# Float32r products that read the two halves of each 128 moving columns in turn

## The chip, the cores and the metric

The kernel runs on one core of one Trainium2 chip. The metric is the device time of one execution in microseconds (us); less is better. TensorE (PE) multiplies, its weight loads are shown apart (PEld), VectorE (DVE), ScalarE (ACT) and GpSimd (POOL) work on elements, and transfers (DMA) are issued from the queues of SyncE (SP) and ScalarE.

## The reference

Sliding-window attention over 8 batches, 8 heads, 576 positions, 64 dimensions a head, followed by a two-layer network with a slope of its own for each hidden unit:

```python
def _attn_ref(q, k, v):
    scores = scale * np.matmul(q, k.transpose(0, 1, 3, 2))
    mask = (rel >= 0) & (rel < 64)
    ...
    return np.matmul(attn, v)

def _moe_ref(x, w_in, w_out, alpha):      # x: 4608 x 512, w_in: 512 x 2048, w_out: 2048 x 512
    h = x @ w_in
    g = np.maximum(h, 0.0) + alpha * np.minimum(h, 0.0)
    return g @ w_out
```

## The kernel before

The 4608 tokens are 36 tiles of 128, worked on in nine blocks of four tiles. Attention gives the tokens `x`, transposed (channels on partitions). The first product, `x @ w_in`, gives `h` with 128 hidden units on the partitions and a block's 512 tokens as columns, one hidden slice `f` of 16 at a time. ScalarE, VectorE and GpSimd make `g` of it. The second product takes 128 tokens of `g` as the stationary operand and a slice of `w_out` (512 output columns) as the moving one, and adds up a tile of the output in a PSUM bank over the 16 slices.

Each of the two operands of a product is held as a float32r number and a float32r rest (names ending in `h` and `l`), and a product is three float32r matmuls: high by high, high by low, low by high. The operands of attention are plain float32.

Five places issue float32r matmuls. `hidden` in `cell` (L1173) does the first product for blocks 0 and 1: twelve matmuls a slice, most of them with 512 moving columns (the tokens), a few with 256. `product` in `pair` (L1305) does it for the blocks behind, in a scheme with seven products of half size in place of eight: the moving operand is 256 tokens. `outs` in `behind` (L852) does the second product for all blocks but the last: 512 moving columns of `w_out`. `products` in `behind_last` (L1023) does the second product of the last block, again with seven products in place of eight, with 256 moving columns. In all of them the moving columns lie one behind the other in the partition's memory, and each matmul has a weight load of its own of 128 columns.

Finished tiles of the output go from PSUM to SBUF in `copy` (L894 on ScalarE, L896 on VectorE) and out in `store` (L899), 32 of them. The last block's four quarters are added up and moved in `quarter`: `make` (L1138 on ScalarE, L1140 on VectorE or GpSimd), with one store each from L1147 (two for the last one).

The order of the work on every engine is fixed ahead: `step` collects steps with their costs, `Plan.order` lays them out by costs and due times, and the instructions are issued in that order. Engines wait for each other by semaphores alone, so an engine that is done early goes on early. The costs in the plan are no part of the change.

Of the kernel before, what the change touches and what calls it, by code (L numbers as in the profile page):

```python
# [14 lines left out]
ALU = mybir.AluOpType  # L15
# [3 lines left out]
PE, DVE, ACT, POOL, SP = "PE", "DVE", "ACT", "POOL", "SP"  # L19
# [99 lines left out]
class Plan:  # L119
# [5 lines left out]
    def step(self, engines, emit, after=(), behind=(), take=(), give=(), want=math.inf, moved=0.0, span=0.0,  # L125
             port=False):

        s = Step(engines, emit, after, list(behind), list(take), list(give), want, moved, span, port)
        for a in s.after + s.behind:
            a.before.append(s)
        s.group = self.group
        self.steps.append(s)
        return s
# [152 lines left out]
def banded_attention_then_prelu_ffn(  # L289
# [11 lines left out]
    nc = tc.nc  # L301
    P = 128
    D = 64
    W = WINDOW
# [50 lines left out]
    def weight(name, f):  # L355
        f0 = max(x for x in parts_of[name] if x <= f)
        return parts_of[name][f0][:, f - f0, :]
# [5 lines left out]
    def tokens_of(x, where):  # L363
        half, start = divmod(where.start, NBLK * P)
        return xs_of[x, half][:, :, start:start + where.stop - where.start]
# [14 lines left out]
    nc.vector.memset(nought, 0.0)  # L380
    plan.idle = lambda _: nc.tensor.matmul(spare, nought, nought, start=True, stop=True)  # L381
    step = plan.step

    def bank(b, shape, dtype, name):
        return ps.tile(shape, dtype, tag=f"b{b.at}", name=name)
# [419 lines left out]
    po = {}  # L805
# [5 lines left out]
    def behind(ts, f, d, done, hb, want_o, cols, coarse=True):  # L811
        n = len(ts)
        nt = n * P
# [7 lines left out]
        start = ts[0] < NBLK  # L821
# [23 lines left out]
        def outs(todo):  # L845
            gh, gl = d["gh"], d.get("gl")
            for i, k in todo:
                t = ts[i]
                if f == 0 and k == 0:
                    po[t] = bank(ob[t], [P, E], F32, f"o_{t}")  # L850
                gt, wt = ((gh, "wout_h"), (gh, "wout_l"), (gl, "wout_h"))[k]
                nc.tensor.matmul(po[t], gt[:, cols[i] * P:(cols[i] + 1) * P], weight(wt, f),  # L852
                                 start=(f == 0 and k == 0), stop=(f == NF - 1 and k == 2))

        hold = {2: (1.46, 0.37, 0.40, 0.31, 0.69), 4: (2.72, 0.57, 0.667, 0.53, 1.24)}[n]
# [1 line left out]
        if f == 0:  # L857
            for t in ts:
# [5 lines left out]
                  give=[hb if start else gb])  # L864
# [3 lines left out]
        for todo in todos:  # L868
# [5 lines left out]
                      give=[ghb] + [glb] * lows, want=want_o)  # L874
# [5 lines left out]
        if f == NF - 1:  # L880
            apart = ts[0] // NBLK == W0 - 1
            if apart:
                old = [Buffer(f"x{i}", NBLK) for i in range(NBLK, RING)]
            for i, t in enumerate(ts):
                for x in parts(t):
                    sbuf, os = Buffer("g" if t == NT - 1 else "gh" if t == NT - 2 else "os", 1), {}

                    def copy(e, t=t, x=x, sbuf=sbuf, os=os, i=i):
                        if apart and not i:
                            lent_of["out"] = sb.tile([P, NP, NBLK * P], F32, tag="xh1", name="lent_out")  # L890
                        os[0] = (lent_of["out"][:, i] if apart else
                                 room(sbuf, [P, x.stop - x.start], F32, f"os_{t}_{x.start}"))
                        if e == ACT:
                            nc.scalar.copy(os[0], po[t][:, x])  # L894
                        else:
                            nc.vector.tensor_copy(os[0], po[t][:, x])  # L896

                    def store(e, t=t, x=x, os=os):
                        (nc.scalar if e == ACT else nc.sync).dma_start(out[t * P:(t + 1) * P, x], os[0])  # L899

                    m = len(parts(t))
                    c = step({DVE: (0.33, 0.42)} if x.start else {ACT: (0.28, 0.39)} if m == 2 else
                             {ACT: (0.48, 0.59), DVE: (0.6, 0.69)}, copy, [whole[t]],
                             [c] if apart and i else [], take=[] if apart and i else old if apart else [sbuf],
                             give=[ob[t]], want=want_o + 3 + i)
                    step({ACT: (0.4, 0.4)} if x.start else {SP: (0.4, 0.4)}, store, [c],
                         give=old if apart else [sbuf], moved=0.8 / m)
                    if t < NBLK:
                        begun.append(c)

    HALF = NF // 2
    entries_o, kept_o, slots, acc, mid = {}, {}, {}, {}, {}
# [49 lines left out]
    def behind_last(ts, f, d, done, hb, want_o, cols):  # L962
        n = NB - 1
        i = f % HALF
# [3 lines left out]
        lh, rh = slice(0, 2 * P), slice(2 * P, 4 * P)  # L968
# [47 lines left out]
        def products(name, kind, gh, gl, w):  # L1016
            fresh = name not in acc
            if fresh:
                acc[name] = bank(acc["b", name], [P, E], F32, f"acc_{name}")
            for j in range(2):  # L1020
                x, y = gh[:, j * P:(j + 1) * P], gl[:, j * P:(j + 1) * P]
                for k, (a, b) in enumerate(((x, w[0]), (x, w[1]), (y, w[0]))):
                    nc.tensor.matmul(acc[name][:, j * 2 * P:(j + 1) * 2 * P], a, b, start=fresh and j == k == 0,  # L1023
                                     stop=k == 2, skip_group_check=True)

        def product(name, kind, gh, gl, w, deps, give):
# [100 lines left out]
        u2 = step(wide, lambda _: sum_u("u2", None, lambda: acc["P6"], lambda: mid["P1"]), [p6], give=[acc["b", "P6"]], want=want_o)  # L1127
        u4 = step(wide, lambda _: sum_u("u4", fb, lambda: acc["P5"], lambda: u["u2"]), [p5, u2], take=[fb], give=[acc["b", "P5"]], want=want_o)
        def quarter(kind, rows, side, x, y, deps, want):
            many = 2 if x is last else 1  # L1130
            b, o = Buffer(kind, many), {}
            where = out[ts[0] * P:].rearrange("(j r p) c -> r p j c", j=2, r=2)[rows][:, :, side]

            def make(e):
                o[0] = room(b, [P, E], F32, f"quarter_{rows}_{side.start}").rearrange("p (j c) -> p j c", j=2)
                o[1] = o[0].rearrange("p j c -> p (j c)")
                if y is None:
                    nc.scalar.copy(o[1], x())  # L1138
                else:
                    (nc.gpsimd if e == POOL else nc.vector).tensor_tensor(out=o[1], in0=x(), in1=y(), op=ALU.add)  # L1140

            c = step({ACT: (0.48, 0.59)} if y is None else {POOL: (1.22, 1.28)} if x is u4_of else wide, make, deps, take=[b], want=want)
            for j in range(many):
                js = slice(j, j + 1) if many == 2 else slice(0, 2)

                def store(e, js=js):
                    (nc.scalar if e == ACT else nc.sync).dma_start(where[:, js], o[0][:, js])  # L1147

                step({ACT: (0.4, 0.4)} if j or rows and side is lh else {SP: (0.4, 0.4)}, store, [c], give=[b], moved=0.8 / many)
            return c  # L1150

        last, u4_of = lambda: acc["P1"], lambda: u["u4"]
# [7 lines left out]
    def cell(ts, f, want_h, want_o):  # L1160
        plan.group = "c", f, ts[0]
        n = len(ts)
        nt = n * P
        d = {}
        xs = slice((ts[0] % RING) * P, (ts[0] % RING) * P + nt)
        hb = Buffer("bank", 1)

        def hidden(_):
            d["h"] = ph = bank(hb, [P, NBLK * P], F32, f"h_{ts[0]}_{f}")
            k = 0  # L1170
            for wt, xt in (("win_h", "h"), ("win_h", "l"), ("win_l", "h")):
                for c in range(NP):
                    nc.tensor.matmul(ph[:, :nt], weight(wt, f)[:, c * P:(c + 1) * P], tokens_of(xt, xs)[:, c],  # L1173
                                     start=(k == 0), stop=(k == 3 * NP - 1))
                    k += 1

        xb = [st[t]["x"] for t in ts]
        s0 = step({PE: ({2: 1.46, 4: 2.72}[n], {2: 1.55, 4: 2.87}[n])}, hidden,
                  [st_done[t] for t in ts] + cv[2 * f]["done"], take=[hb], want=want_h)
        first[ts[0] // NBLK, f] = s0  # L1180
        for b in xb:
            b.uses = NF
        s0.give += xb
        if ts[0] // NBLK == W0 - 1:
            s0.give += regions[f // 2]
        behind(ts, f, d, [s0], hb, want_o, range(n), not (ts[0] // NBLK == W0 - 1 and f >= NF - 2))
# [79 lines left out]
    def pair(ts, q, want):  # L1266
        plan.group = "c", 2 * q, ts[0]
        n = ts[0] // NBLK
        f = 2 * q
# [31 lines left out]
        def product(out, w, x, start):  # L1301
            todo = [(w[i], x[j]) for i, j in ((0, 0), (0, 1), (1, 0))]
            for i, (a, b) in enumerate(todo):
                for c in range(2):
                    nc.tensor.matmul(out, a[:, c * P:(c + 1) * P], b[c], start=start and i == c == 0,  # L1305
                                     stop=i == 2 and c == 1, skip_group_check=True)

        def p12(_):
# [56 lines left out]
        cols = (0, 2, 1, 3)  # L1365
# [10 lines left out]
    for i, rooms in enumerate(TSETS):  # L1376
        b = Buffer(f"reg{i}", 3 * 6, f"T{i}")
# [54 lines left out]
    for n in range(2, NB + 1):  # L1432
        for i in (0, 1):
            m, f = (n - 1, STAYS[1] if n > 2 else 6) if i else (n - 2, STAYS[0]) if n > 2 else (1, 2)
# [93 lines left out]
```

## Time and profile before

| | us |
|---|---|
| three runs | 871.85, 869.1, 871.83 |
| median | 871.83 |
| span of the profiled execution | 869.5 |
| TensorE busy in it | 860.6 |
| VectorE, ScalarE, GpSimd busy | 596.0, 480.7, 425.4 |

The busy time of TensorE takes in the modelled ends of matmuls that overlap, so the rows that count are the times from one start to the next, which the chain of waits gives for a run of matmuls. The granted TensorE clock is 1.00 of its full 2.4 GHz.

### The profile page before, as it was taken

What the parts mean: (1) busy time and instruction counts of PE and PEld (TensorE: products, weight loads), DVE (VectorE), ACT (ScalarE), POOL (GpSimd) and SP (SyncE); (2) the same over time, 40 slices, a digit from 0 to 9 for tenths busy, and PEclk for the clock granted to TensorE, in tenths of its full rate; (3) what the DMA queues carried; (4) which work ended last, traced back from release to release, by engine and by line L of the source; (5) the groups of instructions that cost most, each with busy time, mean ns of one, the idle gap of its engine ahead of it and who ended that gap; (6) DMA issues with size and microseconds to landing.
All of it is one profiled execution on the core that took longest, in us unless ns stands there. A gap on an engine that the chain in (4) does not pass through costs nothing.

```text
span 869.5 us, 21449 instructions
## 1 busy us (share of the span) xinstructions
PE 860.6 (99%) x7937; PEld 765.4 (88%) x7937; DVE 596.0 (69%) x1683; ACT 480.7 (55%) x1290; POOL 425.4 (49%) x422
## 2 busy tenths in 40 slices
PE   9999999999999999999999999999999999999997
PEld 8887778888989898989899889989898989899997
DVE  6888978987775663877585678558776638425655
ACT  7888767447463534664554646364645446434542
POOL 5877656886333324646264435543353433222452
PEclk9999999999999999999999999999999999999999
DMA  9655846565665565766667575767676754367764
GB/s 317 209 185 176 257 162 215 161 213 184 224 183 182 144 190 183 226 188 191 207 184 229 170 241 144 238 179 223 185 230 171 214 185 138 107 204 227 230 202 158
DMA packets 128631, 170.75 MB, mean 196 GB/s; under 512 B 9728, under 2 KB 82448, under 8 KB 128528
## 3 DMA queue, kind: packets, MB, share of 16 engines
q1 hardware_dynamic: 127520, 168.47, 63.2%
q8 instruction: 63, 1.03, 0.5%
q10 hardware_dynamic: 1008, 0.93, 0.3%
q14 instruction: 40, 0.33, 0.1%
HBM read 141.04 MB, written 28.31 MB: 195 GB/s over the span
## 4 chain that ended last, share of the span: by engine, by line
PE 93%; DVE 2%; DMA 2%; ACT 1%; issue 0%; POOL 0%; ACTq 0%; DVEq 0%; SPq 0%; POOLq 0%
PE o L852 39%; PE h L1305 32%; PE h L1173 8%; PE acc_P L1023 4%; PE av L711 4%; PE s L590 3%; DMA raw<-w_in 1%; PE s L572 1%; PE spare L381 1%; DMA raw<-w_out 1%; PE t L668 1%; ACT two L414 0%; DVE two L424 0%; DVE val L433 0%; DVE two L416 0%
## 5 line engine op out<-in xcount | busy, mean ns | idle before, releaser
L835 POOL TENSOR_TENSOR gl<-g,gh 128x512 fp32r<-128x512 f32 x112 | 144.7, 1301 | 221.8 <-ACT gh L831 106.4
L852 PE MATMUL o<-wout_h,gh 128*128 128x512 f32 x512 | 203.4, 397 | 0.0
L852 PE MATMUL o<-wout_l,gh 128*128 128x512 f32 x512 | 201.5, 394 | 0.0
L818 ACT ACTIVATE g<-h,sa_sb 128x512 f32<-128x512 f32 (+1 forms) x132 | 89.2, 676 | 144.4 <-DVE h L1332 121.3
L852 PE MATMUL o<-wout_h,gl 128*128 128x512 f32 x512 | 142.0, 390 | 0.0
L691 DVE STREAM_TRANSPOSE pt<-w 32x256 f32<-32x256 f32 x312 | 128.2, 426 | 5.4 <-POOL w L651 0.7
L852 PEld LDWEIGHTS o<-wout_h,gl 128*128 128x128 f32 x512 | 95.3, 188 | 20.2
L852 PEld LDWEIGHTS o<-wout_h,gh 128*128 128x128 f32 x512 | 96.7, 189 | 17.2 <-issue 0.5
L852 PEld LDWEIGHTS o<-wout_l,gh 128*128 128x128 f32 x512 | 96.7, 189 | 15.1
L825 DVE SCALAR_TENSOR_TENSOR g<-h,s_sb,g 128x512 f32<-128x512 f32 x112 | 84.0, 750 | 37.8 <-ACT g L818 34.9
L1332 DVE TENSOR_TENSOR h<-h,w 128x256 f32<-128x256 f32 x56 | 24.2, 433 | 124.5 <-PE h L1305 124.5
L831 ACT CAST gh<-g 128x512 fp32r<-128x512 f32 x112 | 69.4, 621 | 49.1 <-DVE g L825 48.6
L630 ACT ACTIVATE w<-w,nm 128x96 f32<-128x96 f32 x208 | 76.1, 372 | 14.5 <-DVE nm L624 14.5
L1342 ACT COPY u<-h 128x256 f32<-128x256 f32 x112 | 41.8, 373 | 73.4 <-PE h L1305 69.5
L651 POOL TENSOR_TENSOR w<-w,rc 128x768 f32<-128x768 f32 (+2 forms) x44 | 59.3, 1347 | 46.0 <-DVE rc L647 40.5
L1305 PE MATMUL h<-xh,win_l 128*128 128x256 f32 x336 | 67.6, 283 | 0.0
L1305 PE MATMUL h<-xh,win_h 128*128 128x256 f32 x336 | 65.9, 283 | 0.0
L1305 PEld LDWEIGHTS h<-xh,win_h 128*128 128x128 f32 x336 | 56.7, 189 | 8.0 <-DVE h L1332 0.5
L1305 PE MATMUL h<-win_h,win_l 128*128 128x256 f32 x336 | 60.5, 283 | 0.0
L1332 DVE TENSOR_TENSOR h<-h,u 128x256 f32<-128x256 f32 x112 | 47.7, 428 | 15.8 <-PE h L1305 11.8
L1305 PEld LDWEIGHTS h<-xh,win_l 128*128 128x128 f32 x336 | 53.0, 191 | 0.8
L1305 PEld LDWEIGHTS h<-win_h,win_l 128*128 128x128 f32 x336 | 50.1, 190 | 0.9
(206 smaller groups left out, 1856.5 us busy)
## 6 DMA issues: line engine op xcount, KB each, us to landing
win_h<-kept SPq DMA_DIRECT2D x112, 256.0 KB, 2.9
win_l<-kept SPq DMA_DIRECT2D x112, 256.0 KB, 3.0
v<-vN SPq DMA_DIRECT2D x72, 256.0 KB, 4.4
stream<-kept SPq DMA_DIRECT2D x56, 256.0 KB, 2.8
k<-kT SPq DMA_DIRECT2D x35, 384.0 KB, 4.1
q<-qT SPq DMA_DIRECT2D x34, 256.0 KB, 4.5
raw<-w_in SPq DMA_DIRECT2D x16, 512.0 KB, 5.0
raw<-w_out SPq DMA_DIRECT2D x16, 512.0 KB, 3.7
```

The costliest lines, as they stand in the source:

```text
L630: nc.scalar.activation(w, w, AF.Exp, scale=-1.0, bias=d["nm"][:, g:g + 1], accum_out=d["sm"][:, g:g + 1])
L651: nc.gpsimd.tensor_tensor(out=w, in0=w, in1=d["rc"][:, g].unsqueeze(2).broadcast_to(list(w.shape)), op=ALU.mult)
L691: nc.vector.transpose(dst[:, :, i * SUB:(i + 1) * SUB], d["w"][r, :, :, k * SUB:(k + 1) * SUB].rearrange("p e h k -> p (e h) k"))
L818: nc.scalar.activation(d["g"], d["h"][:, :nt], AF.Copy, scale=sa_sb[:, f:f + 1])
L825: nc.vector.scalar_tensor_tensor(out=g, in0=d["h"][:, :nt], scalar=s_sb[:, f:f + 1], in1=d["g"], op0=ALU.mult, op1=ALU.max)
L831: nc.scalar.copy(d["gh"], d["g"])
L835: (nc.vector if start else nc.gpsimd).tensor_tensor(out=d["gl"], in0=d["g"], in1=d["gh"].bitcast(F32), op=ALU.subtract)
L852: nc.tensor.matmul(po[t], gt[:, cols[i] * P:(cols[i] + 1) * P], weight(wt, f), start=(f == 0 and k == 0), stop=(f == NF - 1 and k == 2))
L1173: nc.tensor.matmul(ph[:, :nt], weight(wt, f)[:, c * P:(c + 1) * P], tokens_of(xt, xs)[:, c], start=(k == 0), stop=(k == 3 * NP - 1))
L1305: nc.tensor.matmul(out, a[:, c * P:(c + 1) * P], b[c], start=start and i == c == 0, stop=i == 2 and c == 1, skip_group_check=True)
L1332: nc.vector.tensor_tensor(out=out, in0=a, in1=b, op=ALU.add)
L1342: nc.scalar.copy(d["u"][i], d[x])
```

## The change

Every moving operand of a float32r matmul is given another order of its columns: of each group of 128 columns the first of the lower 64, the first of the upper 64, the second of the lower 64, the second of the upper 64, and so on (`turned_in`). The bytes read are the same; two columns that follow each other lie 64 elements, 256 bytes, apart. The stationary operands are read as before.

What comes out has its columns in that order. In the first product the columns are tokens, so in `h` and `g` the tokens of each tile stand in turned order; they are the stationary columns of the second product, and so the rows of the output tile are turned. The columns of the output are turned by the moving operand `w_out`. The copies of output tiles (`in_turn` to `turned_in`) put the columns back: they read in a row and write 64 elements apart in turn. The stores (`rows_of`) put the rows back by the order of the rows in DRAM. In the last block each quarter is now stored in two transfers in place of one (the last one had two already).

```diff
+    def turned_in(x):
+        return x.rearrange("p (n a b) -> p n b a", a=2, b=W)
+
+    def in_turn(x):
+        return x.rearrange("p (n b a) -> p n b a", a=2, b=W)
+
+    def rows_of(x):
+        return x.rearrange("(a b) c -> b a c", a=2)
...
-                nc.tensor.matmul(po[t], gt[:, cols[i] * P:(cols[i] + 1) * P], weight(wt, f),
+                nc.tensor.matmul(po[t], gt[:, cols[i] * P:(cols[i] + 1) * P], turned_in(weight(wt, f)),
...
-                            nc.scalar.copy(os[0], po[t][:, x])
+                            nc.scalar.copy(turned_in(os[0]), in_turn(po[t][:, x]))
                         else:
-                            nc.vector.tensor_copy(os[0], po[t][:, x])
+                            nc.vector.tensor_copy(turned_in(os[0]), in_turn(po[t][:, x]))
 
                     def store(e, t=t, x=x, os=os):
-                        (nc.scalar if e == ACT else nc.sync).dma_start(out[t * P:(t + 1) * P, x], os[0])
+                        (nc.scalar if e == ACT else nc.sync).dma_start(rows_of(out[t * P:(t + 1) * P, x]), os[0])
...
-                    nc.tensor.matmul(acc[name][:, j * 2 * P:(j + 1) * 2 * P], a, b, start=fresh and j == k == 0,
+                    nc.tensor.matmul(acc[name][:, j * 2 * P:(j + 1) * 2 * P], a, turned_in(b), start=fresh and j == k == 0,
...
-            many = 2 if x is last else 1
-            b, o = Buffer(kind, many), {}
-            where = out[ts[0] * P:].rearrange("(j r p) c -> r p j c", j=2, r=2)[rows][:, :, side]
+            b, o = Buffer(kind, 2), {}
+            where = out[ts[0] * P:].rearrange("(j r p) c -> r j p c", j=2, r=2)[rows][:, :, side]
...
-                o[1] = o[0].rearrange("p j c -> p (j c)")
+                o[1] = turned_in(o[0].rearrange("p j c -> p (j c)"))
                 if y is None:
-                    nc.scalar.copy(o[1], x())
+                    nc.scalar.copy(o[1], in_turn(x()))
                 else:
-                    (nc.gpsimd if e == POOL else nc.vector).tensor_tensor(out=o[1], in0=x(), in1=y(), op=ALU.add)
+                    (nc.gpsimd if e == POOL else nc.vector).tensor_tensor(
+                        out=o[1], in0=in_turn(x()), in1=in_turn(y()), op=ALU.add)
...
-            for j in range(many):
-                js = slice(j, j + 1) if many == 2 else slice(0, 2)
...
+            for j in range(2):
+                def store(e, j=j):
+                    (nc.scalar if e == ACT else nc.sync).dma_start(rows_of(where[j]), o[0][:, j])
+
+                step({ACT: (0.4, 0.4)} if j or rows and side is lh else {SP: (0.4, 0.4)}, store, [c], give=[b], moved=0.4)
...
-                    nc.tensor.matmul(ph[:, :nt], weight(wt, f)[:, c * P:(c + 1) * P], tokens_of(xt, xs)[:, c],
+                    nc.tensor.matmul(ph[:, :nt], weight(wt, f)[:, c * P:(c + 1) * P], turned_in(tokens_of(xt, xs)[:, c]),
...
-                    nc.tensor.matmul(out, a[:, c * P:(c + 1) * P], b[c], start=start and i == c == 0,
+                    nc.tensor.matmul(out, a[:, c * P:(c + 1) * P], turned_in(b[c]), start=start and i == c == 0,
```

## Rows read from the trace of the kernel before

**Rows 1.** The page: busy time by engine, granted clock, chain that ended last.
```profile
PE 860.6 (99%) x7937; PEld 765.4 (88%) x7937; DVE 596.0 (69%) x1683; ACT 480.7 (55%) x1290; POOL 425.4 (49%) x422
...
PEclk9999999999999999999999999999999999999999
...
PE 93%; DVE 2%; DMA 2%; ACT 1%; issue 0%; POOL 0%; ACTq 0%; DVEq 0%; SPq 0%; POOLq 0%
```

**Rows 2.** Chain in order of time: start us, us, what, count of instructions.
```profile
177.41 8.16 PE h L1173 x36
...
304.45 2.75 PE o L852 x12
...
340.23 2.87 PE h L1305 x24
...
850.66 12.97 PE acc_P L1023 x108
```

**Rows 3.** Groups of TensorE by line: out<-in, shapes, count, busy, mean ns.
```profile
L852 PE MATMUL o<-wout_h,gh 128*128 128x512 f32 x512 | 203.4, 397 | 0.0
...
L1305 PE MATMUL h<-xh,win_l 128*128 128x256 f32 x336 | 67.6, 283 | 0.0
...
L1305 PE MATMUL h<-win_h 128*128 128x256 f32 x84 | 16.9, 282 | 0.0
...
L1173 PE MATMUL h<-xh,win_h 128*128 128x512 f32 x112 | 30.4, 393 | 0.0
...
L1173 PE MATMUL h<-xh,win_h 128*128 128x256 f32 x32 | 5.5, 294 | 0.0
...
L1023 PE MATMUL acc_P<-win_l,g2h 128*128 128x256 f32 x32 | 6.1, 283 | 0.0
...
L1023 PE MATMUL acc_P<-win_l,gl 128*128 128x256 f32 x6 | 1.7, 282 | 0.0
```

**Rows 4.** Timeline (start us, us) and durations (min/median/max) of plain float32 transposes, then float32r loads.
```profile
114.93 0.60 PE L668 MATMUL t<-ident,w 128*128 128x128 f32 x4
...
L668 PEld LDWEIGHTS t<-ident,w x64: 137/140/143, 10.5 to 125.6; 128*128 128x128 f32 x64
L668 PE MATMUL t<-ident,w x64: 270/272/328, 10.5 to 125.7; 128*128 128x128 f32 x64
...
L1305 PEld LDWEIGHTS h<-xh,win_l x336: 187/192/192, 222.8 to 843.7; 128*128 128x128 f32 x168
```

**Rows 5.** Busy time by stretch: us, PE, PEld, DVE, ACT, POOL (counts), clock, DMA.
```profile
226.00:510.00 284.00, 284.00 (x2778) 255.19 (x2777) 189.23 (x559) 145.15 (x406) 120.23 (x127) 1.00 0.65 196
```

**Rows 6.** Waits: engine and line, for whom, us in total, times, longest.
```profile
PE t L668 <- DVE gl L835: 1.6, 1, 1.6
...
DVE h L1332 <- PE h L1305: 136.3, 80, 6.2
```

**Rows 7.** Copies, sums and masks by line: count, ns min/median/max, first and last start.
```profile
L894 ACT COPY os<-o x15: 578/589/605, 132.1 to 789.7; 128x512 f32<-128x512 f32 x15
...
L896 DVE COPY os<-o x13: 691/691/692, 326.2 to 790.2; 128x512 f32<-128x512 f32 x13
...
L614 DVE CUSTOM_DVE_ANT_0 w<-s,masks x80: 259/286/310, 5.7 to 147.9; 128x128 f32<-128x128 f32 x80
...
L624 DVE CUSTOM_DVE_ANT_0 w<-s,masks x184: 247/253/259, 169.1 to 722.9; 128x96 f32<-128x96 f32 x184
```

**Rows 8.** Timeline of the end: ScalarE, VectorE, GpSimd, then SyncE's queue.
```profile
865.10 0.59 ACT L1138 COPY quarter<-acc_P 128x512 f32<-128x512 f32 x1 [6.79 <-DVE quarter L1140]
865.72 0.36 ACTq L1147 DMA_DIRECT2D out<-quarter  x1
...
864.38 0.69 DVE L1140 TENSOR_TENSOR quarter<-acc_P,u 128x512 f32<-128x512 f32 x1
...
863.79 1.30 POOL L1140 TENSOR_TENSOR quarter<-u,pt 128x512 f32<-128x512 f32 x1 [8.32 <-DVE u L1124]
...
865.11 1.49 SPq L1147 DMA_DIRECT2D out<-quarter  x3
```

## What the change was predicted to do

> **What bounds the kernel now.** I read the page first. TensorE is busy for 99% of the span, its clock was granted in full, and 93% of the chain that ended last is TensorE [rows 1]. A busy TensorE need not be TensorE at its peak, so the second question is its pace, and the chain in order of time answers it: a run of matmuls stands there as one piece with its start, length and count, and length over count is the time from one start to the next [rows 2]. L1173 with 512 columns: 8.16 / 36 = 226.7 ns. L852 with 512: 2.75 / 12 = 229.2 ns. L1305 with 256: 2.87 / 24 = 119.6 ns. L1023 with 256: 12.97 / 108 = 120.1 ns. At 2.4 GHz and a column per clock, 512 columns are 213.3 ns and 256 are 106.7 ns. So each matmul carries a surplus of 13 to 16 ns that no wait explains. Third, the waits: the longest in which TensorE waited for an engine is 1.6 us in one place, while VectorE waits 136.3 us for TensorE in L1332 alone [rows 6]. TensorE's pace is the kernel's pace, and a change to how a matmul reads its columns acts on the path directly.
>
> **How much surplus there is.** The counts are in [rows 3]: L852 has three groups of 512, so 1,536; L1173 three of 112 with 512 columns and three of 32 with 256; L1305 eleven groups from 336 to 84, 2,352 in all; L1023 twenty groups from 32 to 6, 336 in all. Surplus: 1,536 x 15.9 = 24.4 us, 336 x 13.4 = 4.5 us, 2,352 x 12.9 = 30.3 us, 336 x 13.4 = 4.5 us, 96 x 12.9 = 1.2 us (L1173's few taken at L1305's pace). Sum 64.9 us, 7.5% of the span. No order of reading can win more, unless it also makes a column cost less than a clock.
>
> **What of it the order can move.** No row shows a moving operand read in two places, so this is bounded from both sides. The nearest row for the good end is the plain float32 transpose: four of them in 0.60 us, the last one 0.272 us long, so (600 - 272) / 3 = 109.3 ns from start to start [rows 4]. That is 128 columns at two clocks each, 106.7 ns, and a surplus of only 2.6 ns, though it loads 128 weight columns for each matmul as the float32r ones do. So changing weights does not cost 13 ns by itself. The surplus appears where four bytes per partition are wanted every clock, and that looks like a feed that cannot quite keep up. Reading two places in turn could let one be fetched while the other is used. With the surplus down to 2.6 ns, a 512-column matmul saves 13.3 ns in L852 and 10.8 ns in L1173, and a 256-column one 10.3 ns in L1305 and 10.8 ns in L1023.
>
> The other feed is the weight load, and it is not touched: it still reads its columns in a row. A float32r load takes 192 ns at the median in L1305, and the transposes' load 140 ns [rows 4], so it has a surplus of its own. Beside a 512-column matmul there is room for it. Beside a 256-column one a load is under way nearly all the time, and it may be the load that sets the 119.6 ns. For the 512-column ones I therefore take the whole saving: 1,536 x 13.3 + 336 x 10.8 = 24.0 us. For the 256-column ones the ends are nothing and 2,352 x 10.3 + 336 x 10.8 + 96 x 10.3 = 28.8 us; no row is nearer to one end, and I take half, 14.4 us. Together 38.4 us.
>
> **What is lost on the way.** Only 93% of the chain is TensorE [rows 1]; the rest is mostly the start, where weights arrive. Saving counts there in part: 38.4 x 0.93 = 35.7 us. Next late: in the stretch of 284 us from 226 us on, VectorE is busy for 189.2 us and the transfers' share is 0.65 [rows 5]; with TensorE 4% faster that is 69% and 0.68, so neither becomes the bound as a total. But the products of a pair hang on copies and sums between them, whose length stays. The order of work was laid out for today's pace, and some of those answers will come late. The ends are nothing and a third of the gain, 12 us; I take a tenth, 3.5 us, as the waits of today are so small. That leaves 32.2 us.
>
> **Outputs.** The 32 copies (ScalarE 0.589 us, VectorE 0.691 us [rows 7]) and the four quarters now write 64 elements apart in turn. The nearest row is a VectorE mask written two elements apart: 286 ns for 128 columns against 253 ns for 96 written in a row, so 33 / 32 = 1.03 ns a column, which shows no price for a small step [rows 7]. A large step is not shown: bounds are nothing and double the time. The 32 copies lie beside matmuls, and TensorE never waited for one [rows 6]; if they cost double, some bank of output comes free 0.6 us later at a block's start, behind other products. At the end they are on the path: VectorE, then ScalarE's last copy of 0.59 us at 865.10, then the last stores [rows 8]; doubled, about 2 us. The quarters' stores go from five to eight. SyncE's queue issues three as before; ScalarE's goes from two to five, at about 0.4 us each [rows 8]. Stores that stand ahead of the last copy in ScalarE's queue wait for GpSimd's and VectorE's sums, which end at 865.1, and hold that copy back. The bound is 0 to 1.6 us for the issues. For the whole end I take 0.6 us, nearer to the lower bound, as the small step cost nothing. The rows of a store keep their length, and `h`, `g` and the casts work on columns in whatever order, so the rest of the edits is free.
>
> **The sum.** 32.2 - 0.6 = 31.6 us. The profiled execution spans 869.5 us, so 837.9 us. The median of the three runs, 871.8 us, stands 2.3 us above that span, and I add the same: 840 us. The forecast's own range: all 52.8 us saved and nothing lost gives 869.5 - 52.8 + 2.3 = 819 us; the 512-column saving alone, with 8 us lost behind it, gives 856 us.
>
> **Rivals.** *The order changes nothing.* The surplus may arise behind the read, in the array, or in the weight load, which stays as it is. For it: the float32r load is longer than the other load [rows 4]. Against: L1173 with 512 columns has room for the load and still carries 13.4 ns [rows 2]. Then only the end counts: 871.8 + 0.6 = 872 us, 871 to 874.
>
> *Each column costs a fetch of its own (slower).* Today neighbours in memory follow each other, and one fetch may serve several columns. In turn, no two that follow each other are neighbours. If the reader keeps only one place at hand, each column waits for its own fetch. The nearest row for a column that comes every second clock is again the transpose, 109.3 ns for 128 [rows 4]: 437 ns for 512 columns, 219 for 256. Added: 1,536 x 208 + 336 x 210 + 2,352 x 99 + 336 x 99 + 96 x 99 = 666 us, so about 1,538 us. It decides from the point where a turned 512-column matmul takes more than today's 229.2 ns. Against it: a reader that holds two places at once has the same neighbours at hand as before. No row decides between one and two.
>
> [...]
>
> *The two places collide with the weight load (a little slower).* Two streams from the moving operand and one from the weights meet more often than one and one. If the surplus grows by half, 64.9 / 2 = 32 us are added, 904 us; if it doubles, 937 us. For it: the same 512 columns take 226.7 ns in L1173 and 229.2 ns in L852 [rows 2], so something besides the count already acts on the pace.
>
> **How the numbers follow.** Forecast 0.62, no effect 0.14, a fetch per column 0.13, collisions 0.11. The predicted time is the forecast's, 840 us. The range goes from 819 us to 905 us: it holds the forecast but for a few hundredths, the second case, and half of the collisions, and leaves out the fetch per column, about 0.2 in all. Of the changes, 0.3% (2.6 us) is about what a measurement of this kernel can tell from none. Faster takes the forecast, 0.62; the same takes the case of no effect, 0.14; slower the two others, 0.24.
>
> **What would show it.** In the chain of the changed kernel a run of 12 in L852 should be near 2.59 us (215.9 ns each), against 2.75 for no effect and over 5 for a fetch per column. The 24 of L1305 should fall between 2.62 and 2.87 us; at 2.87 the weight load sets their pace. L668, which is not changed, must stay at 109 ns. Waits of TensorE for VectorE and ScalarE (L1332, L1342) should appear, some 4 us in all; if they come to over 12 us, the plan's order gives the gain back. The copies of L894 and L896 should stay near 0.59 and 0.69 us. The prediction is wrong in kind if a turned 512-column matmul takes as long as today or longer.

## The result and the profile after

The changed kernel takes 840.2 us (median of four runs, 838.6 to 840.9) against 871.8 us before: ratio 0.964, 95% interval 0.962 to 0.966. The profiled execution spans 836.6 us, against 869.5 us. The change adds nine lines ahead of the loops, so L852 of before is L861 now, L1173 is L1180, L1305 is L1312 and L1023 is L1032.

The page after, with the rows that answer to [rows 1]:

```profile
PE 820.9 (98%) x7937; PEld 746.4 (89%) x7937; DVE 606.5 (72%) x1683; ACT 491.3 (59%) x1290; POOL 423.1 (51%) x422
...
PE 81%; DVE 6%; DMA 6%; ACT 5%; issue 1%; POOL 1%; ACTq 0%; DVEq 0%; POOLq 0%
```

As many matmuls, at the same clock (mean 0.999), take 33 us less. But the chain that ended last is TensorE for 81% now and was for 93%, and the waits of TensorE that the profile lists come to 8.9 us in place of 4.3: TensorE waits more often. The pace stands in the chain in order of time (start us, us, what, count), as in [rows 2]:

```profile
174.72 7.77 PE h L1180 x36
...
255.98 2.01 PE h L1312 x18
...
329.10 2.59 PE o L861 x12
...
817.30 10.73 PE acc_P L1032 x96
```

With 512 columns L1180 takes 7.77 / 36 = 215.8 ns and L861 2.59 / 12 = 215.8 ns; with 256, L1312 takes 2.01 / 18 = 111.7 ns and L1032 10.73 / 96 = 111.8 ns. The difference between L1173 and L852 in [rows 2] is gone. The copies, by line (count, ns min/median/max), with [rows 7] to compare:

```profile
L903 ACT COPY os<-o x15: 1061/1087/1164, 131.5 to 759.9; 128x512 f32<-128x512 f32 x15
...
L905 DVE COPY os<-o x13: 1061/1082/1095, 317.7 to 760.6; 128x512 f32<-128x512 f32 x13
```

ScalarE's went from 0.589 to 1.087 us, VectorE's from 0.691 to 1.082 us. The end, in the timelines of TensorE's last matmul (before, then now), ScalarE, VectorE and SyncE's queue, answers to [rows 8]:

```profile
864.78 0.28 PE L1023 MATMUL acc_P<-wout_h,g1l 128*128 128x256 f32 x1
...
830.42 0.28 PE L1032 MATMUL acc_P<-wout_h,g1l 128*128 128x256 f32 x1
...
831.38 1.04 ACT L1146 COPY quarter<-acc_P 128x512 f32<-128x512 f32 x1 [6.93 <-PE acc_P L1032]
831.40 2.56 ACTq L1154 DMA_DIRECT2D out<-quarter  x4
...
830.46 1.12 DVE L1148 TENSOR_TENSOR quarter<-acc_P,u 128x512 f32<-128x512 f32 x1
...
830.94 2.04 SPq L1154 DMA_DIRECT2D out<-quarter  x3
```

TensorE's last matmul starts at 864.78 us in the timeline of before and at 830.42 us in this one, 34.4 us earlier, and the span is 32.9 us shorter: the end has become 1.5 us longer.

### The profile page after: what moved, and what is told of

The parts are those of the page before. It is cut to its first block, busy times and chain, and to the rows that moved or that the text cites. A ratio compares the mean times of both kernels' runs of the same rounds, so it can differ in the third digit from the quotient of the medians.

```text
span 836.6 us, 21452 instructions
## 1 busy us (share of the span) xinstructions
PE 820.9 (98%) x7937; PEld 746.4 (89%) x7937; DVE 606.5 (72%) x1683; ACT 491.3 (59%) x1290; POOL 423.1 (51%) x422
## 4 chain that ended last, share of the span: by engine, by line
PE 81%; DVE 6%; DMA 6%; ACT 5%; issue 1%; POOL 1%; ACTq 0%; DVEq 0%; POOLq 0%
PE o L861 33%; PE h L1312 29%; PE h L1180 6%; PE acc_P L1032 4%; PE av L720 4%; PE s L599 3%; DMA raw<-w_in 2%; DMA out<-os 1%; DVE pt L700 1%; DMA raw<-w_out 1%; PE s L581 1%; ACT low L438 1%; ACT two L423 1%; PE spare L381 1%; DMA win_h<-kept 1%
## 5 line engine op out<-in xcount | busy, mean ns | idle before, releaser
L861 PE MATMUL o<-wout_h,gh 128*128 128x512 f32 x512 | 197.3, 385 | 0.2
L861 PE MATMUL o<-wout_l,gh 128*128 128x512 f32 x512 | 194.1, 379 | 0.0
L861 PE MATMUL o<-wout_h,gl 128*128 128x512 f32 x512 | 136.0, 379 | 0.0
L861 PEld LDWEIGHTS o<-wout_h,gh 128*128 128x128 f32 x512 | 97.1, 190 | 13.0 <-ACT lent_out L903 0.5
L861 PEld LDWEIGHTS o<-wout_h,gl 128*128 128x128 f32 x512 | 95.9, 189 | 13.1
L861 PEld LDWEIGHTS o<-wout_l,gh 128*128 128x128 f32 x512 | 97.2, 190 | 9.3
L1349 ACT COPY u<-h 128x256 f32<-128x256 f32 x112 | 41.8, 373 | 52.9 <-PE h L1312 49.3
L1312 PE MATMUL h<-xh,win_l 128*128 128x256 f32 x336 | 64.9, 275 | 0.0
L1312 PE MATMUL h<-xh,win_h 128*128 128x256 f32 x336 | 63.6, 277 | 0.6 <-DVE h L1339 0.5
L1312 PEld LDWEIGHTS h<-xh,win_h 128*128 128x128 f32 x336 | 55.1, 190 | 7.8 <-DVE h L1339 1.4
L1312 PE MATMUL h<-win_h,win_l 128*128 128x256 f32 x336 | 59.7, 281 | 0.0
L1312 PEld LDWEIGHTS h<-xh,win_l 128*128 128x128 f32 x336 | 51.8, 192 | 0.5
L1312 PEld LDWEIGHTS h<-win_h,win_l 128*128 128x128 f32 x336 | 50.0, 191 | 0.9
```

Of the source, the lines that this page charges most:

```text
L1312: nc.tensor.matmul(out, a[:, c * P:(c + 1) * P], turned_in(b[c]), start=start and i == c == 0, stop=i == 2 and c == 1, skip_group_check=True)
L1349: nc.scalar.copy(d["u"][i], d[x])
```

## The experiments

Four kernels take the change apart, four change the order of the columns, and four ask about what is left. Ratios are to runs of the kernel before on the same chip (870.7 us for the first four, 869.6 us for the next four, 871.2 us for the last four). All are variants of the changed kernel, and the diffs stand against it, those of the five column orders and of m_half_load against e3_products_only; `...` marks what is left out of a diff. The five that change the order of the columns, m_half_load and v_read_side were executed once each.

**The second product alone.**

```diff
-  ... turned_in(tokens_of(xt, xs)[:, c]), ...      # first product, L1180
+  ... tokens_of(xt, xs)[:, c], ...
-  ... a[:, c * P:(c + 1) * P], turned_in(b[c]), ...   # first product, L1312
+  ... a[:, c * P:(c + 1) * P], b[c], ...
-  dma_start(rows_of(out[t * P:(t + 1) * P, x]), os[0])
+  dma_start(out[t * P:(t + 1) * P, x], os[0])
...
```

> Only the second product (L852, L1023 of before) reads its columns in turn, with the copies that put the output's columns back; the first product and the rows of the stores are as before. Theory (the surplus belongs to the moving read of each matmul): L852 goes to 216 ns and L1023 to 111.5 ns, L1173 and L1305 stay at 227 and 119.5 ns; saving 1,536 x 13.2 + 336 x 8.4 = 23 us, less some 7 us for the doubled copies and late answers: 856 us (852 to 860). Rival (the surplus is a collision between a matmul's read and the next one's weight load, whoever is turned): the lines that are not turned change their pace too, and this half brings over 30 us or under 10 us.

852.7 us, ratio 0.980 (0.978 to 0.981), in the theory's range. The chain's pieces:

```profile
175.41 8.19 PE h L1180 x36
183.60 5.18 PE o L861 x24
...
219.77 2.15 PE h L1312 x18
...
831.45 10.73 PE acc_P L1032 x96
```

L861 and L1032 go to 215.8 and 111.8 ns; L1312 stays at 2.15 / 18 = 119.4 ns and L1180 at 227.5 ns.

**The first product alone.** The opposite: `turned_in` in L1180 and L1312 only, `rows_of` in the stores, copies as before.

```diff
-  ... turned_in(weight(wt, f)), ...                # second product, L861
+  ... weight(wt, f), ...
-  ... a, turned_in(b), start=fresh ...             # second product, L1032
+  ... a, b, start=fresh ...
-  nc.scalar.copy(turned_in(os[0]), in_turn(po[t][:, x]))
+  nc.scalar.copy(os[0], po[t][:, x])
...
```

> Only the first product (L1173, L1305 of before) reads its columns in turn, with the stores that put the rows back; copies write in a row, quarters keep two stores each. Theory: L1305 goes to 111.5 ns and L1173 to 216 ns, L852 and L1023 stay at 229 and 120 ns; saving 2,352 x 7.8 + 336 x 12 + 96 x 8 = 23 us, less some 4 us for late answers: 853 us (849 to 857). Rival (collision with weight loads): L852 changes its pace too, or L1305 does not reach 111.5 ns while L852 is not turned.

856.2 us, ratio 0.984 (0.982 to 0.985), in the theory's range.

```profile
184.15 5.47 PE o L861 x24
189.62 5.18 PE h L1180 x24
...
248.32 2.01 PE h L1312 x18
...
266.06 2.79 PE o L861 x12
...
834.79 12.96 PE acc_P L1032 x108
```

Again only what is turned goes faster; L861 in its later pieces is even a little slower, 2.79 us for 12 against 2.75 in [rows 2], some 3 ns each. The two halves save 18.0 and 14.4 us, 32.4 together; the whole saves 31.7. The surplus belongs to the moving read of each matmul; the rival, in which it comes from a neighbour's load or read, falls but for those 3 ns.

**The products without the output's order.** Copies, stores and the function `quarter` are those of before.

```diff
-  nc.scalar.copy(turned_in(os[0]), in_turn(po[t][:, x]))
+  nc.scalar.copy(os[0], po[t][:, x])
-  nc.vector.tensor_copy(turned_in(os[0]), in_turn(po[t][:, x]))
+  nc.vector.tensor_copy(os[0], po[t][:, x])
-  dma_start(rows_of(out[t * P:(t + 1) * P, x]), os[0])
+  dma_start(out[t * P:(t + 1) * P, x], os[0])
...
```

> All products read in turn; copies, quarters and stores are those of the kernel before. It leaves out putting rows and columns of the output back in order. Theory A (most of what the faster matmuls do not bring to the end is lost to the copies, which take 1.08 us in place of 0.59 and 0.69, and to the end): 834 us (832 to 837). Theory B (it is lost to answers that come late since the order was laid out for the old pace): 839 us (838 to 840), only the end's 1.5 us come back.

834.8 us, ratio 0.959 (0.958 to 0.960), in the range of theory A. The profiled execution spans 833.9 us; its start is taken up below:

```profile
176.44 7.77 PE h L1182 x36
```

**The output's order without the products.** The diff is the other half: all four matmul lines read in a row again, everything else stays.

```diff
-  ... turned_in(weight(wt, f)), ...
+  ... weight(wt, f), ...
...
```

> Products as before, copies and stores turned; the output is in another order, since only one side of the change is made. Theory A (the doubled copies cost at the block boundaries, where TensorE or ScalarE's other work waits behind them): 875 us (873.5 to 878). Theory B (copies hidden beside matmuls, only the end counts): 873 us (872 to 873.5).

877.1 us, ratio 1.008 (1.006 to 1.009), 6.4 us longer and in the range of theory A. The chain around a block's start in this kernel shows how the outputs can cost time; its first row here is the 36 matmuls of [rows 2], its last one TensorE's last piece:

```profile
178.84 8.16 PE h L1180 x36
...
328.05 1.12 DVE os L905
...
329.18 2.40 DMA out<-os
...
331.65 0.04 ACT os L903
...
332.53 0.45 ACT u L1349
332.97 0.98 ACT os L903
333.95 0.22 ACT w L1347
...
334.22 1.70 PE h L1312 x12
...
854.75 12.97 PE acc_P L1032 x108
```

VectorE's copy takes 1.12 us, its store 2.40 us more; only then is the buffer free for which ScalarE's next copy waits. In ScalarE's order, fixed ahead, the copies of the next pair stand behind output copies: L1349, at 332.53 us, behind the one that starts at 331.65 us, and L1347, at 333.95 us, behind the one that starts at 332.97 us. L1312 on TensorE waits for them and goes on at 334.22 us. The same pieces stand in the chain of the changed kernel from 317.65 to 323.76 us. TensorE's last piece starts 4.1 us later than in [rows 2], of the 5.4 us by which this profiled span (874.9 us) is longer. But 1.4 us of that stand there already at the 36 matmuls (178.84 against 177.41 us), and as much at the same run's first showing (134.21 against 132.79 us), where the first output copy only begins (133.6 us). So 4.0 us are the outputs' in this execution: 2.7 us beside matmuls, 1.3 us at the end. A copy that lies beside matmuls is only hidden as long as what is queued behind it on its engine is not wanted.

**Other orders.** Four kernels with the products alone turned, as in e3_products_only, and one line changed:

```diff
     def turned_in(x):
-        return x.rearrange("p (n a b) -> p n b a", a=2, b=W)
+        return x.rearrange("p (n a b) -> p n b a", a=2, b=2)      # m_same_line
+        return x.rearrange("p (n a b) -> p n b a", a=2, b=4)      # m_next_line
+        return x.rearrange("p (n a b) -> p n b a", a=64, b=2)     # m_step2
+        return x.rearrange("p (n a b) -> p n b a", a=32, b=4)     # m_step4
```

> As the kernel with the products alone turned, but the order is columns 0, 2, 1, 3 of each four, 8 bytes apart, within 16 bytes; the output's order is left out. Two-places theory (the read gains when columns that follow each other come from two separate pieces of memory): nothing is gained, 512 columns stay at 227 to 230 ns, 256 at 119.5 ns, some 870 us. Rival (any order that isn't one column behind the other gains): 216 and 111.5 ns, 835 us.

870.8 us, against 869.6 us of before.

> Order 0, 4, 1, 5, 2, 6, 3, 7 of each eight: two places in turn, only 16 bytes apart; the output's order is left out. Two-places theory with any distance: 216 and 111.5 ns, 835 us. Rival (the distance matters, the 256 bytes of the change fall into another part of the memory than their neighbour, 16 bytes do not): 227 and 119.5 ns or slower, 870 us or more.

829.8 us.

> Order 0, 2, 4 ... 126, 1, 3 ...: one place, walked in steps of two columns (8 bytes), so that two columns in a row share 16 bytes; the output's order is left out. Two-places theory: no gain, 227 and 119.5 ns or somewhat slower, 870 us or more. Rival (any order that isn't one behind the other): 216 and 111.5 ns, 835 us.

1,589.7 us.

> Order 0, 4, 8 ... 124, 1, 5 ...: one place, walked in steps of four columns (16 bytes), so that each column begins a new 16 bytes and comes back to it only 32 columns later; the output's order is left out. A fetch per column (the slower rival of the prediction, tested where nothing can be kept at hand): 437 ns or more for 512 columns, 1,500 us or more. Two-places theory without a price for a fetch: 227 ns, 870 us. Rival (the read is short only when columns share 16 bytes): 216 ns, 835 us.

1,616.8 us.

The pace, from the chain in order of time, of m_same_line, m_next_line, m_step2 and m_step4 in that order:

```profile
177.06 8.16 PE h L1182 x36
```

```profile
172.42 7.77 PE h L1182 x36
```

```profile
298.64 16.32 PE h L1182 x36
```

```profile
681.53 5.60 PE h L1314 x24
```

Columns 0, 2, 1, 3, which stay within 16 bytes, take 226.7 ns for 512: nothing is gained. Two places 16 bytes apart take 215.8 ns, the same as two places 256 bytes apart. One place walked in steps of two columns takes 16.32 / 36 = 453 ns, and in steps of four 5.60 / 24 = 233 ns for 256 columns: half the pace. That m_step2 runs at half pace neither of its two theories had foreseen. So it is not the row that has to be broken, nor does the distance matter between the two that were tried. Two places in turn lose all but 2.5 ns of the surplus, though columns that follow each other lie 16 or 256 bytes apart; one place in steps is far worse, though in steps of two they lie 8 bytes apart.

**Four places in turn**, 128 bytes apart: the same line with `a=4, b=32`.

> Products alone, four places in turn, 32 columns (128 bytes) apart; the output's order is left out. Theory (the read keeps exactly two pieces of 16 bytes at hand): every column finds its piece gone, half pace or worse as in steps of four columns, 450 ns for 512 columns, some 1,590 us. Rival (it keeps four or more): 216 and 111.5 ns, 830 to 835 us.

1,002.0 us.

```profile
199.63 9.84 PE h L1182 x36
...
253.06 2.49 PE h L1314 x18
```

273 ns for 512 columns and 138 ns for 256: slower than in a row, but far from half pace. Neither the theory of exactly two pieces at hand nor the rival of four fits.

**Half the weight load** in L1312 (it has another number here).

```diff
+                    m = P if i == c == 0 else P // 2
-                    nc.tensor.matmul(out, a[:, c * P:(c + 1) * P], turned_in(b[c]), ...
+                    nc.tensor.matmul(out[:m], a[:, c * P:c * P + m], turned_in(b[c]), ...
```

> Products alone turned, and in L1305 of before all but the first matmul of each product load 64 weight columns in place of 128 and write 64 rows; it leaves out half of the hidden units of the later blocks and the output's order. Theory (the weight load beside it sets the 111.5 ns of a turned 256-column matmul): 109 ns there, some 5 us less than with whole loads. Rival (111.5 ns is the matmul's own): it stays at 111 to 112 ns.

831.2 us.

```profile
255.89 1.97 PE h L1315 x18
```

1.97 / 18 = 109.4 ns, against 111.7 ns with whole loads. This run halves the rows written together with the load, so it alone does not say which of the two counts. The changed kernel speaks for the load: by the start times in its trace, the first L1312 behind an L861, whose load of 128 columns has ended by then, takes 109 ns with all 128 rows written, and those behind it, which start while their load still runs, take 111 to 112 ns. The load then sets the last 2.3 ns, and no more. From those 109 ns to the 215.8 ns of 512 columns it is 106.8 ns for 256 more columns, 0.417 ns each: the traces give the clock as a share of full speed alone, but this pace bears out the 106.7 ns that the prediction took for 256 columns. What then remains of the 109.4 ns above them is 2.7 ns, about the surplus of the transposes in [rows 4]. The total is no proof: it is 3.6 us below e3_products_only, but m_next_line, with whole loads and on the same chip as this run, took 829.8 us.

**The copy reads in turn and writes in a row** (ScalarE's alone; VectorE's and the quarters as in the change).

```diff
-  nc.scalar.copy(turned_in(os[0]), in_turn(po[t][:, x]))
+  nc.scalar.copy(os[0].rearrange("p (n a b) -> p n a b", a=2, b=W),
+                 po[t][:, x].rearrange("p (n b a) -> p n a b", a=2, b=W))
```

> As the changed kernel, but ScalarE's copies of output tiles read PSUM in turn and write in a row, where the change reads in a row and writes in turn. Theory (ScalarE has to go to two places for columns that follow each other, whichever side): 1.09 us as in the change. Rival (only writing in turn is dear): 0.59 us. The whole stays within 837 to 841 us.

835.1 us, in one run: below the 837 to 841 us that were expected. The profiled execution spans 833.1 us.

```profile
175.07 7.77 PE h L1180 x36
...
L903 ACT COPY os<-o x15: 581/589/603, 131.8 to 756.6; 128x512 f32<-128x512 f32 x15
```

The rival holds: ScalarE reads PSUM in steps of two columns at no price, and pays only for writing 64 elements apart in turn. VectorE's copies still write so and take 1.081 us each, and yet the kernel is no slower than the next one, which has all its copies short.

**Columns laid out ahead.** `w_out` is rearranged on the host, so that reading it in turn gives the output's columns in their natural order. Copies and quarters write in a row, stores still put the rows back.

```diff
-        "w_out": np.ascontiguousarray(moe_w_out).view(np.int64),
+        "w_out": np.ascontiguousarray(moe_w_out.reshape(-1, E // P, W, 2).transpose(0, 1, 3, 2))
+                 .reshape(-1, E).view(np.int64),
...
```

> As the changed kernel, but w_out's columns are laid out on the host so that reading them in turn gives the output's columns in their natural order; copies and quarters write in a row again, stores still put the rows back. Theory (the doubled copies cost some 5 us, the stores' new row order next to nothing): 835 us (833.5 to 837), copies at 0.59 and 0.69 us again. Rival (the stores' order, or the two stores for each quarter, is what costs): 838.5 to 840 us.

836.3 us, ratio 0.960 (0.958 to 0.962). The copies are back at 0.589 and 0.691 us. The profiled execution spans 835.9 us; in its chain stand the 36 matmuls again, and at the same block's start TensorE alone:

```profile
178.11 7.77 PE h L1180 x36
...
318.70 2.59 PE o L861 x12
321.30 2.01 PE h L1312 x18
323.31 0.87 PE o L861 x4
324.17 2.06 PE h L1312 x18
```

By the medians it is 3.9 us less than the changed kernel, which was timed on another occasion; the intervals of the two ratios just touch at 0.962. So, but for the end of the kernel, the row order of the stores costs little, and the columns' order in the copies is what costs.

## Why the prediction was right, point by point

**The bound.** TensorE's pace set the time, as read from [rows 1, 2, 6]: a pace 5.8% better at 512 columns and 6.6% better at 256 made the kernel 3.6% faster.

**The 512-column term** was 24.0 us, from the transposes' surplus of 2.6 ns. Measured: 1,536 x 13.4 + 336 x 10.9 = 24.2 us. The surplus went to 215.8 - 213.3 = 2.5 ns. The step from [rows 4], that what a slower reader does not lose is what the order can win, held to a tenth of a nanosecond, and the 12 of L852 take the 2.59 us that were named as its sign. The size was in part luck: the 0.60 us of [rows 4] are given to a hundredth, which leaves nearly 2 ns either way on the 109.3. The 213.3 ns for 512 columns are twice 106.7 ns; 256 more columns take 226.7 - 119.6 = 107.1 ns in [rows 2] and 106.8 ns in the changed kernel. The two clocks for a column of the transposes were the author's estimate from the 109.3 ns for 128 columns, 0.854 ns each; no other width of them was measured.

**The 256-column term** was mis-sized. Half of 28.8 us was taken, 14.4 us, since the weight load might be the bound. Measured: 2,352 x 7.9 + 336 x 8.3 + 96 x 7.9 = 22.1 us, three quarters. m_half_load, with the changed kernel's trace, speaks for the load as what sets the pace beside 256 columns, as suspected from [rows 4], but at 111.7 ns and not near 119.6; the 24 of L1312 take 2.73 us, between the 2.62 and 2.87 us that were named.

**What is lost on the way** was mis-sized the other way, and so the forecast of 840 us came out to the microsecond by luck, by two errors that cancel. Predicted were 2.7 us at the start, 3.5 us of late answers and 0.6 us at the end, 6.8 us in all. Measured: 46.3 us of pace (24.2 + 22.1; the start times of all matmuls that nothing held up give 46.2) brought 32.9 us of span, so 13.4 us were lost. The same 36 matmuls start at 177.41 us in [rows 2] and at 174.72 us now, 2.7 us earlier. Ahead of them stand 276 matmuls of L852 and 229 of L1173 with 512 columns and 96 with 256, which by their pace give 3.7 + 2.5 + 0.8 = 7.0 us: 4.3 us lost. From there to the last matmul 31.7 us came of the other 39.3: 7.6 us lost. The end lost 1.5 us.

**The outputs** are the step that failed. The copies were put between no price and double, and 0.6 us was taken for the whole end since a step of two elements was free in [rows 7]. That step was no guide to one of 64: the copies take 1.85 and 1.57 times as long. That they were hidden beside matmuls was read from waits of today, which are small [rows 6]. From the start of the 36 matmuls to the end of the span it is 836.6 - 174.72 = 661.9 us in the changed kernel, 657.8 us in v_layout, 658.0 us in v_read_side and 657.5 us in e3_products_only. So the copies cost some 4 us of the 13.4, by way of ScalarE's queue: v_read_side gets them back with ScalarE's copies alone. With the old products the outputs cost 4.0 us over the same stretch (e4_outputs_only). These are single executions, and m_next_line, with the copies of e3_products_only and the same pace, needs 655.7 us, so the 4 us are good to about 2. So part of what was put down to late answers belongs to the copies. At the very end it is the stores: from the last matmul's start to the end it is 4.7 us in the kernel before, 6.2 us in the changed one and still 5.9 us in v_layout, whose copies and quarters are short.

**The rest of the loss** stays open. From the 36 matmuls to the last one v_layout gains (864.78 - 177.41) - (829.94 - 178.11) = 35.5 us of 39.3, so 3.8 us are lost there with short copies too. That is near the 3.5 us taken for late answers, but no run shows that it is these; the waits of L1312 for ScalarE and VectorE that the profile of the changed kernel lists come to 1.5 us, not to the 4 us that were named as a sign. The 4.3 us of the start are no firm figure: kernels whose matmuls have one pace reach the same 36 matmuls between 172.42 us (m_next_line) and 178.11 us (v_layout), which is most of why m_next_line came out 5 us under the 835 us expected of it; those with the old pace reach them between 177.06 us (m_same_line) and 178.84 us (e4_outputs_only). In the chains of m_next_line and v_layout loads of `w_in` and `w_out` stand ahead of them. What decides between them was not tried.

**The rivals.** No effect: the order acts, and the weight load explains 2.3 ns. A fetch per column: it did not come, but a price of that size exists. m_step2 and m_step4 run at half pace, 1,590 and 1,617 us, where the prediction priced this rival at 1,538 us from the transposes' row. Columns that lie apart are not enough for it: two places in turn, 16 or 256 bytes apart, take 215.8 ns for 512 columns, faster than in a row. Columns that lie close do not keep it away: steps of two columns, 8 bytes, take 453 ns. Collisions with the load: no turned matmul is slower for them; only matmuls read in a row beside turned neighbours lost a little, L861 in e2_first_only some 3 ns and L1180 in e1_second_only about 1 ns.

**Why two places help** is shown only from outside. A reader with two pieces at hand, which fetches one while it uses the other, is in keeping with the paces in a row, in turn and of m_same_line; the like pace of m_step2 and m_step4, and m_four with 273 ns, don't follow from it. The mechanism stays open.

## What to carry to other kernels

When a chain is all TensorE, compare the time from one matmul's start to the next, for each shape, with what the columns alone take by the difference of two shapes (107.1 ns for 256 columns in [rows 2]); here float32r matmuls had a surplus that the plain float32 transposes lacked, and reading two places in turn took it from 13 to 16 ns down to 2.5 ns at 512 columns (226.7 and 229.2 ns to 215.8 ns). Put the order back where it costs least, in the layout of an operand ahead of time or, away from the kernel's end, in the rows of a store, and not in a copy that writes apart in turn (on ScalarE 1.087 us in place of 0.589). Before a longer copy is called hidden, see what stands behind it in its engine's queue, and who waits for that.

## What the runs showed of the hardware

- At a granted clock of 0.998 to 1.00 a float32r matmul takes 226.7 ns (L1173) or 229.2 ns (L852) for 512 columns read in a row, 215.8 ns from two places in turn (16 or 256 bytes apart), 273 ns from four places (128 bytes apart), 453 ns from one place in steps of two columns.
- ScalarE and VectorE write 128x512 float32 in turn, 256 bytes apart, in 1.087 and 1.082 us; in a row in 0.589 and 0.691 us. ScalarE reads PSUM two columns apart and writes in a row in 0.589 us. GpSimd's sum takes 1.296 us either way (L1140 before, L1148 now).
- Beside float32r weight loads of 128 columns a turned 256-column matmul takes 111.7 ns; with loads of 64 columns, and 64 rows written, it takes 109.4 ns. In the changed kernel the first one behind a run of 512-column matmuls, with its load over before it starts, takes 109 ns.
